# Decay sums by a prefix scan, first rows copied inside SBUF, later rows asked for an iteration ahead

## The chip, the cores and the metric

The kernel runs on one core of one Trainium2 chip. The metric is the device time of one execution in microseconds (us); a verdict compares medians of runs. TensorE (PE) does matmuls, with its weight loads in a queue of their own (PEld); VectorE is DVE, ScalarE is ACT, GpSimd is POOL. SyncE (SP) issues all DMAs here, in program order, one after the other.

## The reference

```python
scores = scale * np.matmul(q, k.transpose(0, 1, 3, 2))      # B=4, H=8, S=576, D=64
cum = np.cumsum(np.log(np.clip(f, 0.0001, 1.0)), axis=-1)
scores = np.where(causal, -1e9, scores + cum[:, :, :, None] - cum[:, :, None, :])
attn = softmax(scores)                                      # with 1e-9 in the denominator
x = (attn @ v), heads side by side                          # 2304 x 512
x = np.maximum(x @ w_in, 0.0) ** 2 @ w_out                  # d_ff 2048
out = (sigmoid(x @ w_gate) * (x @ w_val)) @ w_out2          # d_ff 1536
```

All inputs are float32; the running sum `cum` along the 576 positions of each of the 32 heads is the "decay sum" of the title. A row constant drops out of a softmax, so only `cum` of the key's position has to be added to the scores.

## The kernel before

The work has an attention part and, behind it, four passes of large matmuls for the two feed-forward layers. The attention part handles the 32 heads as 16 pairs. Each float32 operand of a matmul is split into a high and a low part (`qh`, `ql`, `kh`, `kl`), and a score block is the sum of `ql·kh`, `qh·kl`, `qh·kh` and of a fourth matmul that multiplies ones (`one_l`) with the tile `cr`: its rows 0, 1 and 64, 65 hold the high and low part of `cum` of the two heads. So no score block is complete before `cr` of its pair is there. `cr` exists twice, for even and odd pairs.

`setup()` runs once. It loads `f`, clips it (DVE), takes the logarithm (ACT, which then loads another table for Exp), and makes the running sum on TensorE: five transposes of `f` into `fT` (L242), then 14 matmuls with a triangle of ones (L256), evacuated in two pieces into `cum_s` (L261, L262), high and low. `cum_s` is written to `cum_d` in DRAM (L265). `cum_s`, `f_sb` and the triangle lie inside `pts`, a tile that later holds transposed probabilities.

A table, `ORDER`, fixes what every engine does in one iteration: each word is a step and a lag. `S01+0` are the first scores of this iteration's pair; `TQ-1` and `TK-1` transpose q and k of the next pair (L270); `qh`, `ql`, `kh`, `kl` split them on ACT and DVE; `R` (row minimum, DVE), `X` (exponential, ACT), `M` (scaling, POOL), `G` (transposes of the probabilities, PE), `E` (their evacuation) and `PV+2` (the product with v, L439) follow over the next two iterations. `TQ` and `TK` also issue the loads of q and k two pairs ahead, `PV` that of v three pairs ahead. `kh-1` issues the two DMAs that bring `cr` of the next pair from `cum_d` (L356): behind the loads of its own iteration on SP. The loads of v of pairs 0 to 2 are issued before the first iteration. A DMA on SP also waits for the DMA eight places ahead of it.

Of the kernel before, what the change touches and what calls it, by code (L numbers as in the profile page):

```python
# [9 lines left out]
F32 = mybir.dt.float32  # L10
F32R = mybir.dt.float32r
I32 = mybir.dt.int32
AF = mybir.ActivationFunctionType
ALU = mybir.AluOpType
# [26 lines left out]
def kernel(  # L41
# [13 lines left out]
    nc = tc.nc  # L55
    B, H, S, D = q.shape
    NT, DM = out.shape
    BH = B * H
    NP = BH // 2
    PB = H // 2  # L60
    NF = S // 128
    REM = S - NF * 128
    NC = NF + 1
# [6 lines left out]
    PC = S + 128 - REM  # L70
    POFF = [128 * (i * (i + 1) // 2) for i in range(NF + 1)]
# [4 lines left out]
    while t0 < NT:  # L76
        n = min(512, NT - t0)
# [5 lines left out]
    cum_d = dram.tile([BH, 2, S], F32, name="cum_d")  # L83
# [61 lines left out]
    def conv_load(n):  # L145
        for key, m, _, _ in conv_q[:n]:
            if (key, m) not in wraw:
                w_load(key, m)

    def conv_some(n):  # L150
        for _ in range(min(n, len(conv_q))):
            w_conv(*conv_q.pop(0))
            conv_load(3)
# [7 lines left out]
    def tiles(n, name, shape, dt=F32):  # L161
        return [ap_.tile(shape, dt, name=f"{name}{i}") for i in range(n)]

    nat = {nm_: tiles(3 if nm_ == "v" else 2, nm_ + "n", [128, NC, 2, D]) for nm_ in "qkv"}
    qk = [{nm_: ap_.tile([128, S], F32R, name=f"{nm_}{i}") for nm_ in ("qh", "ql", "kh", "kl", "cr")} for i in range(2)]
# [3 lines left out]
    pt_t = tiles(2, "pt", [128, 2 * POFF[NF] + PC])  # L169
    pts = ap_.tile([128, 2 * PW + 128], F32, name="pts")  # L170
    sm_t = tiles(2, "sm", [128, 9])
    nm_t = tiles(2, "nm", [128, 9])
    ident = ap_.tile([128, 128], F32, name="ident")
    MD = S + 384
    maskc = ap_.tile([128, MD + 128], F32, name="maskc")
    one_l = ap_.tile([128, 256], F32R, name="one_l")
    ones_f = pts[:, 0:S]
    f_sb = pts[0:BH, S:2 * S]
    cum_s = pts[0:BH, 2 * S:4 * S].bitcast(F32R)
    ones_u = qk[1]["kh"][:, 0:S]  # L180
    fT = qk[1]["kl"][:, 0:2 * NC * BH].rearrange("p (t c) -> p t c", t=2)

    ring = [0]

    def ps2():
        ring[0] += 1
        return pair_t[(ring[0] - 1) % 4]

    def load(p, which):
        b, h0 = divmod(2 * p, H)  # L190
        for src, nm_ in ((q, "q"), (k, "k"), (v, "v")):
            if nm_ not in which:
                continue
            t = nat[nm_][p % len(nat[nm_])]
            for i in range(2):
                nc.sync.dma_start(  # L196
                    out=t[:, 0:NF, i, :],
                    in_=src[b, h0 + i, 0:NF * 128, :].rearrange("(c p) d -> p c d", p=128),
                )
            nc.sync.dma_start(  # L200
                out=t[0:REM, NF, :, :],
                in_=src[b, h0:h0 + 2, NF * 128:S, :].rearrange("h p d -> p h d"),
            )

    def setup():
        nc.sync.dma_start(out=f_sb, in_=f.rearrange("b h s -> (b h) s"))
        for p in range(2):
            load(p, "qk")
        make_identity(nc, ident)
        nc.gpsimd.memset(ones_f, 1.0)  # L210
        nc.gpsimd.affine_select(
            out=ones_f, in_=ones_f, pattern=[[1, S]], compare_op=ALU.is_ge, fill=0.0, base=0, channel_multiplier=-1
        )
        for nm_ in "qkv":
            for t in nat[nm_]:
                nc.gpsimd.memset(t[64:128, NF, :, :], 0.0)
        nc.vector.tensor_copy(ones_u, ones_f)
        for d in qk:
            for nm_ in ("cr", "eh", "el"):
                nc.gpsimd.memset(d[nm_].bitcast(F32), 0.0)  # L220
        for t in pt_t:
            nc.gpsimd.memset(t[:, 2 * POFF[NF] + S:2 * POFF[NF] + PC], 0.0)
        nc.gpsimd.memset(one_l.bitcast(F32), 0.0)
        for r in range(2):
            nc.gpsimd.memset(one_l.bitcast(F32)[64 * r:64 * r + 2, 128 * r:128 * r + 128], 1.0)
        nc.gpsimd.memset(maskc, 0.0)
        nc.gpsimd.affine_select(
            out=maskc[:, MD:MD + 128], in_=maskc[:, MD:MD + 128], pattern=[[-1, 128]],
            compare_op=ALU.is_ge, fill=BIG, base=0, channel_multiplier=1,
        )  # L230
        for r in range(2):
            nc.gpsimd.affine_select(
                out=maskc[64 * r:64 * r + 64, S - REM:S], in_=maskc[64 * r:64 * r + 64, S - REM:S],
                pattern=[[-1, REM]], compare_op=ALU.is_ge, fill=BIG, base=0, channel_multiplier=1,
            )
        nc.vector.tensor_scalar(f_sb, f_sb, 1.0e-4, 1.0, op0=ALU.max, op1=ALU.min)
        nc.scalar.activation(out=f_sb, in_=f_sb, func=AF.Ln)
        nc.scalar.activation(out=sm_t[0][0:BH, 0:1], in_=f_sb[:, 0:1], func=AF.Exp)
        fps = ps2()
        for c in range(NC):  # L240
            n = 128 if c < NF else REM
            nc.tensor.transpose(fps[0:n, c * BH:(c + 1) * BH], f_sb[:, c * 128:c * 128 + n], ident[0:BH, 0:BH])  # L242
        for n, w0, w1 in ((128, 0, NF * BH), (REM, NF * BH, NC * BH)):
            nc.scalar.activation(out=fT[0:n, 0, w0:w1], in_=fps[0:n, w0:w1], func=AF.Copy)
            nc.vector.tensor_tensor(
                out=fT[0:n, 1, w0:w1], in0=fps[0:n, w0:w1], in1=fT.bitcast(F32)[0:n, 0, w0:w1], op=ALU.subtract
            )
        for a, e in ((0, 256), (256, S)):
            cps = ps2()
            for c in range(NC):  # L250
                n = 128 if c < NF else REM
                s = max(a, c * 128)
                if s >= e:
                    continue
                for t in range(2):
                    nc.tensor.matmul(  # L256
                        cps[0:BH, s - a:e - a], lhsT=fT[0:n, t, c * BH:(c + 1) * BH],
                        rhs=ones_u[0:n, s - c * 128:e - c * 128],
                        start=(c == 0 and t == 0), stop=(t == 1 and c == min(NF, (e - 1) // 128)),
                    )  # L260
            nc.scalar.activation(out=cum_s[:, a:e], in_=cps[0:BH, 0:e - a], func=AF.Copy)  # L261
            nc.vector.tensor_tensor(  # L262
                out=cum_s[:, S + a:S + e], in0=cps[0:BH, 0:e - a], in1=cum_s.bitcast(F32)[:, a:e], op=ALU.subtract
            )
        nc.sync.dma_start(out=cum_d, in_=cum_s.bitcast(F32).rearrange("p (t s) -> p t s", t=2))  # L265

    def transpose_in(t):
        x = ps2()
# [83 lines left out]
    def kh(p):  # L352
        d = qk[p % 2]
        nc.scalar.activation(out=d["kh"], in_=live["k", p], func=AF.Copy)
        for h in range(2):
            nc.sync.dma_start(out=d["cr"].bitcast(F32)[64 * h:64 * h + 2, :], in_=cum_d[2 * p + h, :, :])  # L356

    def kl(p):
        d = qk[p % 2]
# [87 lines left out]
    def x_part(p, low):  # L447
# [8 lines left out]
                nc.scalar.activation(out=x[:, 0, xs], in_=i, func=AF.Copy)  # L456

    STEP = {
        "TQ": TQ, "qh": qh, "ql": ql, "EH": EH, "EL": EL, "TK": TK, "kh": kh, "kl": kl,
        "S01": S01, "S2": S2, "S3": S3, "S4": S4, "PV": PV,  # L460
        "xhi": lambda p: x_part(p, 0), "xlo": lambda p: x_part(p, 1),
        "N0": lambda p: N(p, 0, 4), "N2": lambda p: N(p, 4, 6), "N3": lambda p: N(p, 6, 9),
    }
    for c in range(9):
        t = "4" if c == 8 else f"{c // 2}{'ab'[c % 2]}"
        for nm_, fn in (("R", R), ("X", expsum), ("M", M)):
            STEP[nm_ + t] = lambda p, fn=fn, c=c: fn(p, c)
    for g in range(1, 5):
        STEP[f"G{g}"] = lambda p, g=g: G(p, g)
        STEP[f"E{g}"] = lambda p, g=g: E(p, g)  # L470
    ORDER = """
        S01+0 M2a+1 X4+1 M1b+1 E3+2 R0a+0 R1b+0 X3b+1 PV+2 R0b+0 R1a+0 TQ-1 M2b+1 X3a+1
        xhi+2 S2+0 N3+1 qh-1 X0a+0 G1+1 M3b+1 X1b+0 xlo+2 TK-1 E1+1 ql-1 M3a+1 kh-1
        R2b+0 S4+0 X1a+0 X0b+0 R2a+0 X2a+0 G2+1 kl-1 G3+1 R4+0 E2+1 M4+1 EH-1 N0+0
        X2b+0 G4+1 E4+1 N2+0 S3+0 EL-1 M0b+0 M0a+0 M1a+0 R3b+0 R3a+0
# [2 lines left out]
    for m in range(2):  # L478
        conv_q.append(("in", m, ws_p, "wi"))

    setup()
    order = tc.manual_schedule()
    order.__enter__()
    for p in range(3):
        load(p, "v")
    steps = [(w[:-2], int(w[-2:])) for w in ORDER]
    lags = [lag for _, lag in steps]
    for it in range(min(lags), NP + max(lags)):
        for nm_, lag in steps:
            p = it - lag  # L490
            if 0 <= p < NP:
                STEP[nm_](p)
        if it == NP - 4:
            conv_load(2)
        if it in (NP, NP + 1):
            conv_some(1)
# [19 lines left out]
    def up(key, m, j):  # L516
        t0, n = blks[j]
        w = whl[key, m]
        h = hbank()
        for c in range(KD):  # L520
            x = xT[c][:, :, t0:t0 + n]
            wh, wl = w[:, 0, c * 128:(c + 1) * 128], w[:, 1, c * 128:(c + 1) * 128]
            for i, (a, b_) in enumerate(((wh, 0), (wh, 1), (wl, 0))):
                nc.tensor.matmul(  # L524
                    h[:, 0:n], lhsT=a, rhs=x[:, b_, :], start=(c == 0 and i == 0), stop=(c == KD - 1 and i == 2)
                )
        return h[:, 0:n]
# [11 lines left out]
    for m in range(M1):  # L539
        for j, (t0, n) in enumerate(blks):  # L540
            h = up("in", m, j)
# [109 lines left out]
```

## Time and profile before

| | us |
|---|---|
| three runs | 1053.26, 1053.84, 1054.04 (median 1053.84) |
| profiled execution, span from first to last instruction | 1051.2 |
| PE busy in it | 1027.0 |
| DVE / ACT / POOL busy | 503.3 / 399.5 / 220.7 |
| attention part, roughly | 0 to 209 of the span |

The profile has no time of its own beside its span; the median of the runs lies 2.64 us above the span. Read a row of the timeline as: start, duration (from the first of a merged group to the end of the last), engine, line, operation, out<-in, shape, count, and in brackets how long the engine had been idle and for what. A chain of waits is the work followed back from the last instruction to what released it.

### The profile page before, as it was taken

Reading aid. Unit: us, or ns where it says so; the run is one execution under the profiler, and the core shown is the slowest. Engines: PE = TensorE matmul, PEld = TensorE weight load, DVE = VectorE, ACT = ScalarE, POOL = GpSimd, SP = SyncE. Lnnn points to the kernel's source line nnn. Section 1 sums busy time; section 2 is a strip of 40 time slices with the busy share of each in tenths; the row PEclk is TensorE's granted clock in tenths of the full one; section 3 lists DMA queues with packets and bytes.
Section 4 is the critical chain, followed back from the end, with each engine's and each line's share of the span. In section 5 each row is a group of like instructions: output and inputs, shape, how many; then the busy total and the mean of one; then the engine's idle time right before and its main releaser. Section 6 shows DMA issues by size and latency. Waiting matters only on the chain.

```text
span 1051.2 us, 15632 instructions
## 1 busy us (share of the span) xinstructions
PE 1027.0 (98%) x5675; PEld 859.7 (82%) x5675; DVE 503.3 (48%) x1067; ACT 399.5 (38%) x854; POOL 220.7 (21%) x306
## 2 busy tenths in 40 slices
PE   4999999899999999999999999999999999999998
PEld 3788788588888888888888988888888888888887
DVE  2878778597666675233232414444444421232222
ACT  2888778544444343233232323222222211122222
POOL 3776666532122211000000002111111120000000
PEclk7999999899999999999999999999999999999999
DMA  5333333066765565333332214434433211244333
GB/s 121 71 86 87 70 83 106 21 187 199 210 211 188 188 204 167 101 93 98 101 93 83 85 51 119 132 124 132 132 119 107 94 46 46 78 138 140 99 123 110
DMA packets 125965, 121.98 MB, mean 116 GB/s; under 512 B 63552, under 2 KB 91200, under 8 KB 125888
## 3 DMA queue, kind: packets, MB, share of 16 engines
q1 hardware_dynamic: 125888, 120.99, 38.6%
q8 instruction: 44, 0.72, 0.3%
q14 instruction: 33, 0.27, 0.1%
HBM read 83.06 MB, written 37.90 MB: 115 GB/s over the span
## 4 chain that ended last, share of the span: by engine, by line
PE 95%; SPq 2%; DMA 1%; DVE 0%; issue 0%; ACT 0%; POOL 0%; POOLq 0%
PE ps L524 47%; PE ps L588 33%; PE pa L439 4%; PE pa L306 4%; PE pa L405 3%; PE pa L270 2%; PE pa L379 2%; SPq L196 1%; DMA cr<-cum_d 1%; PE pa L411 1%; SPq L200 1%; POOL pt L394 0%; ACT pt L292 0%; SPq L356 0%; ACT pts L316 0%
## 5 line engine op out<-in xcount | busy, mean ns | idle before, releaser
L524 PE MATMUL ps<-xT,hl 128*128 128x512 f32 (+1 forms) x2400 | 494.4, 368 | 0.0
L524 PEld LDWEIGHTS ps<-xT,hl 128*128 128x128 f32 x2400 | 418.4, 189 | 75.8
L141 POOL TENSOR_TENSOR hl<-wf,hl 128x512 fp32r<-128x512 f32 x68 | 93.1, 1377 | 565.1 <-ACT hl L140 548.6
L562 DVE TENSOR_TENSOR gg<-gi,gg 128x512 fp32r<-128x512 f32 (+1 forms) x140 | 90.5, 647 | 237.0 <-ACT gg L561 236.9
L588 PE MATMUL ps<-gg,hl 128*128 128x512 f32 (+1 forms) x960 | 197.3, 368 | 0.0
L588 PEld LDWEIGHTS ps<-gg,hl 128*128 128x128 f32 x960 | 167.2, 189 | 30.0
L561 ACT ACTIVATE gg<-gi 128x512 fp32r<-128x512 f32 (+1 forms) x140 | 82.4, 589 | 251.1 <-PE ps L588 227.8
L588 PE MATMUL ps<-hl,gg 128*128 128x512 f32 x648 | 147.1, 389 | 0.0
L588 PEld LDWEIGHTS ps<-hl,gg 128*128 128x128 f32 x648 | 121.6, 188 | 25.2
L394 POOL TENSOR_TENSOR pt<-pt,sm 128x128 f32<-128x128 f32 (+2 forms) x144 | 105.8, 767 | 53.8 <-DVE sm L389 53.8
L616 DVE TENSOR_TENSOR r<-ps,r 128x512 f32<-128x512 f32 (+1 forms) x60 | 38.2, 636 | 138.1 <-PE ps L524 133.3
L292 ACT ACTIVATE pt<-pt,nm 128x128 f32<-128x128 f32 (+1 forms) x144 | 82.5, 583 | 10.1 <-DVE nm L284 10.0
L137 DVE SCALAR_TENSOR_TENSOR wf<-wraw,wtmp 128x512 int32<-128x512 int32 x68 | 57.6, 848 | 57.4 <-POOL hl L141 56.0
L614 ACT ACTIVATE r<-ps 128x512 f32<-128x512 f32 (+1 forms) x60 | 32.9, 548 | 122.5 <-PE ps L524 122.5
L140 ACT ACTIVATE hl<-wf 128x512 fp32r<-128x512 f32 x68 | 42.9, 631 | 88.6 <-DVE wf L137 47.2
L131 ACT ACTIVATE wtmp<-wraw 128x512 f32<-128x512 f32 x68 | 45.2, 666 | 74.5 <-DMA wraw<-in_moe_w_in_dram 23.4
L284 DVE CUSTOM_DVE_ANT_0 pt<-pa,maskc 128x128 f32<-128x128 f32 (+2 forms) x144 | 67.0, 514 | 12.0 <-PE pa L306 11.4
L543 ACT ACTIVATE r<-ps 128x512 f32<-128x512 f32 (+1 forms) x80 | 42.5, 547 | 43.2 <-DMA g<-r 38.2
L544 DVE TENSOR_TENSOR r<-r 128x512 f32<-128x512 f32 (+1 forms) x80 | 50.7, 646 | 17.0 <-ACT r L543 17.0
L439 PE MATMUL pa<-pts,vn 128*64 128x320 f32 (+4 forms) x448 | 49.2, 371 | 3.9 <-ACT pts L316 3.9
L439 PEld LDWEIGHTS pa<-pts,vn 128*64 128x64 f32 x448 | 30.5, 141 | 22.9 <-ACT pts L316 4.4
L134 DVE SCALAR_TENSOR_TENSOR wtmp<-wraw,wtmp 128x512 int32<-128x512 int32 x68 | 48.0, 708 | 2.2
(79 smaller groups left out, 685.4 us busy)
## 6 DMA issues: line engine op xcount, KB each, us to landing
g<-r SPq DMA_DIRECT2D x112, 256.0 KB
gi<-g SPq DMA_DIRECT2D x112, 256.0 KB
wraw<-in_moe_w_out_dram SPq DMA_DIRECT2D x28, 512.0 KB
wraw<-in_moe_w_in_dram SPq DMA_DIRECT2D x16, 512.0 KB
wraw<-in_moe_w_gate_dram SPq DMA_DIRECT2D x12, 512.0 KB
wraw<-in_moe_w_val_dram SPq DMA_DIRECT2D x12, 512.0 KB
out_dram<-r SPq DMA_DIRECT2D x18, 256.0 KB
qn<-in_q_dram SPq DMA_DIRECT2D x32, 128.0 KB
```

The costliest lines, as they stand in the source:

```text
L134: nc.vector.scalar_tensor_tensor(out=xi, in0=hi, scalar=-0x40000000, in1=xi, op0=ALU.bitwise_and, op1=ALU.bitwise_or)
L137: nc.vector.scalar_tensor_tensor(out=t.bitcast(I32), in0=lo, scalar=29, in1=xi, op0=ALU.logical_shift_right, op1=ALU.bitwise_or)
L141: nc.gpsimd.tensor_tensor(out=hl[:, 1, :], in0=t, in1=hl.bitcast(F32)[:, 0, :], op=ALU.subtract)
L284: nc.vector.tensor_tensor_reduce(out=o, in0=s, in1=mask, scale=1.0, scalar=3.0e38, op0=ALU.add, op1=ALU.min, accum_out=nm_t[p % 2][:, c:c ...
L292: nc.scalar.activation(out=x, in_=x, func=AF.Exp, bias=nm_t[p % 2][:, c:c + 1], scale=-1.0, accum_out=sm_t[p % 2][:, c:c + 1])
L394: nc.gpsimd.tensor_tensor(out=x, in0=x, in1=sm_t[p % 2][:, c:c + 1].to_broadcast([128, e - a]), op=ALU.mult)
L439: nc.tensor.matmul(o[64 * h:64 * h + 64, 512 * half + s - lo:512 * half + hi - lo], lhsT=vn[:, c, h, :], rhs=pts[:, h * PW + c * PS + s:h ...
L524: nc.tensor.matmul(h[:, 0:n], lhsT=a, rhs=x[:, b_, :], start=(c == 0 and i == 0), stop=(c == KD - 1 and i == 2))
L544: nc.vector.tensor_tensor(out=r, in0=r, in1=r, op=ALU.mult)
L561: nc.scalar.activation(out=gg[:, 0, 0:n], in_=t, func=AF.Copy)
L562: nc.vector.tensor_tensor(out=gg[:, 1, 0:n], in0=t, in1=gg.bitcast(F32)[:, 0, 0:n], op=ALU.subtract)
L588: nc.tensor.matmul(o, lhsT=lhsT, rhs=rhs, start=(k_ == 0 and x == 0), stop=(last and x == 2))
```

## The change

Four things change.

The running sum is one DVE instruction: `tensor_tensor_scan` along the 576 positions of the 32 partitions, into `cum_f`, with the clamped logarithms as both operands. ACT copies it to the high half of `cum_s`, DVE subtracts for the low half. The transposes of `f`, the 14 matmuls, the triangle of ones and their evacuations are gone.

`cr` of pairs 0 and 1 is copied from `cum_s`, inside SBUF, in `cr_load`, with one DMA for the high rows of both heads and one for the low rows; it still leaves on SP. For later pairs a new step `CR-1` stands at the head of `ORDER` and reads `cum_d`; `kh` no longer issues these DMAs.

v of pairs 0 to 2 is loaded at the head of iterations 0 to 2. Clearing of tiles that are needed later (`eh`, `el` of the odd pairs, v, the probabilities) moves to `setup_late()`, called at the head of iteration 0. And `setup()` now stands inside the hand-written order, so that its instructions keep their written order too.

```diff
-        for p in range(2):
-            load(p, "qk")
...
+        load(0, "qk")
+        nc.vector.tensor_scalar(f_sb, f_sb, 1.0e-4, 1.0, op0=ALU.max, op1=ALU.min)
+        nc.scalar.activation(out=f_sb, in_=f_sb, func=AF.Ln)
+        nc.scalar.activation(out=sm_t[0][0:BH, 0:1], in_=f_sb[:, 0:1], func=AF.Exp)
+        nc.vector.tensor_tensor_scan(out=cum_f, data0=f_sb, data1=f_sb, initial=0.0, op0=ALU.add, op1=ALU.min)
+        nc.scalar.activation(out=cum_s[:, 0:S], in_=cum_f, func=AF.Copy)
+        nc.vector.tensor_tensor(
+            out=cum_s[:, S:2 * S], in0=cum_f, in1=cum_s.bitcast(F32)[:, 0:S], op=ALU.subtract
+        )
...
+        load(1, "q")
+        cr_load(0, cum_v)
+        load(1, "k")
+        cr_load(1, cum_v)
+        nc.sync.dma_start(out=cum_d, in_=cum_v)
...
-            nc.tensor.transpose(fps[0:n, c * BH:(c + 1) * BH], f_sb[:, c * 128:c * 128 + n], ident[0:BH, 0:BH])
...
-                        cps[0:BH, s - a:e - a], lhsT=fT[0:n, t, c * BH:(c + 1) * BH],
...
+    def cr_load(p, source):
+        d = qk[p % 2]
+        for t in range(2):
+            nc.sync.dma_start(out=d["cr"].bitcast(F32)[t:t + 65:64, :], in_=source[2 * p:2 * p + 2, t, :])
...
     def kh(p):
         d = qk[p % 2]
         nc.scalar.activation(out=d["kh"], in_=live["k", p], func=AF.Copy)
-        for h in range(2):
-            nc.sync.dma_start(out=d["cr"].bitcast(F32)[64 * h:64 * h + 2, :], in_=cum_d[2 * p + h, :, :])
...
-    for p in range(3):
-        load(p, "v")
...
+        if it == 0:
+            setup_late()
+        if 0 <= it < 3:
+            load(it, "v")
```

On SP, the stretch that ends with the first `cr` before. `vn` and `qn`, `kn` are the tiles of v, q and k; 228 to 230 are v of pairs 0 to 2, 224 and 226 belong to even pairs, 225 and 227 to odd ones; `cr_235` is that of even pairs. Ahead of the first row stand `f`, q and k of pairs 0 and 1 and v of pair 0.

```order
L196 DMA vn_229<-in_v_dram 128x4x64 x2
L200 DMA vn_229<-in_v_dram 64x2x64
L265 DMA cum_d<-pts 32x1152
L196 DMA vn_230<-in_v_dram 128x4x64 x2
L200 DMA vn_230<-in_v_dram 64x2x64
L196 DMA qn_224<-in_q_dram 128x4x64 x2
L200 DMA qn_224<-in_q_dram 64x2x64
L196 DMA kn_226<-in_k_dram 128x4x64 x2
L200 DMA kn_226<-in_k_dram 64x2x64
L356 DMA cr_235<-cum_d 2x576 x2
```

The same queue after the change, from q of pair 1 on. Ahead of the first row stand `f` and q and k of pair 0.

```order
L194 DMA qn_225<-in_q_dram 128x4x64 x2
L198 DMA qn_225<-in_q_dram 64x2x64
L206 DMA cr_235<-pts 2x576 x2
L194 DMA kn_227<-in_k_dram 128x4x64 x2
L198 DMA kn_227<-in_k_dram 64x2x64
L206 DMA cr_240<-pts 2x576 x2
L235 DMA cum_d<-pts 32x1152
L194 DMA qn_224<-in_q_dram 128x4x64 x2
L198 DMA qn_224<-in_q_dram 64x2x64
L194 DMA kn_226<-in_k_dram 128x4x64 x2
L198 DMA kn_226<-in_k_dram 64x2x64
L194 DMA vn_228<-in_v_dram 128x4x64 x2
```

The first `cr` moved from behind 29 loads and stores to behind 10; in its old place it also stood behind `cum_d`, from which it reads.

On PE, the head of the program before, up to the first scores of pair 0 (`pa` are PSUM tiles).

```order
L242 MATMUL pa_217<-ident,pts 128x32 x4
L242 MATMUL pa_217<-ident,pts 64x32
L270 MATMUL pa_220<-ident,qn_224 128x128 x3
L256 MATMUL pa_218<-kh_238,kl_239 32x256 x2
L256 MATMUL pa_218<-kh_238,kl_239 32x128 x2
L256 MATMUL pa_219<-kh_238,kl_239 32x320 x6
L256 MATMUL pa_219<-kh_238,kl_239 32x192 x2
L256 MATMUL pa_219<-kh_238,kl_239 32x64 x2
L270 MATMUL pa_220<-ident,qn_224 128x128 x2
L270 MATMUL pa_217<-ident,kn_226 128x128 x5
L306 MATMUL pa_218<-kh_233,ql_232 128x128 x2
```

And after the change.

```order
L262 MATMUL pa_217<-ident,qn_224 128x128 x5
L262 MATMUL pa_218<-ident,kn_226 128x128 x5
L298 MATMUL pa_219<-kh_233,ql_232 128x128 x2
L298 MATMUL pa_219<-kl_234,qh_231 128x128 x2
L298 MATMUL pa_219<-kh_233,qh_231 128x128 x2
L298 MATMUL pa_219<-cr_235,one_l 128x128 x2
```

The transposes of q of pair 0 are no longer cut in two by the matmuls of the running sum, and those of k follow at once.

## Rows read from the trace of the kernel before

**Rows 1.** The page, part 1: busy time of PE, share, instructions.

```profile
PE 1027.0 (98%) x5675; PEld 859.7 (82%) x5675; DVE 503.3 (48%) x1067; ACT 399.5 (38%) x854; POOL 220.7 (21%) x306
```

**Rows 2.** Waits, PE's and SP's: us in total, times, longest us.

```profile
PE pa L306 <- DMA cr<-cum_d: 10.4, 5, 8.7
...
SPq L196 <- PE pa L439: 66.0, 13, 7.7
```

**Rows 3.** Windows: us, busy of PE, PEld, DVE, ACT, POOL, clock, DMA share, GB/s.

```profile
12.00:20.00 8.00, 0.00 (x0) 0.00 (x0) 0.00 (x0) 0.00 (x0) 0.00 (x0) 0.52 0.71 161
20.00:26.00 6.00, 5.49 (x29) 4.53 (x30) 2.98 (x13) 1.52 (x5) 0.93 (x4) 0.50 0.21 48
```

**Rows 4.** Timeline of SP's queue, 0 to 20 us.

```profile
1.26 0.96 SPq L196 DMA_DIRECT2D qn<-in_q_dram  x2
...
3.02 1.14 SPq L196 DMA_DIRECT2D kn<-in_k_dram  x2
...
6.03 0.60 SPq L200 DMA_DIRECT2D qn<-in_q_dram  x1
...
18.34 0.74 SPq L356 DMA_DIRECT2D cr<-cum_d  x2
```

**Rows 5.** Timeline of ACT, DVE and PE, 0 to 21 us.

```profile
3.22 0.68 ACT L237 ACTIVATE pts<-pts 32x576 f32<-32x576 f32 x1 [1.13 <-DVE pts L236]
3.92 1.28 ACT L238 ACT_TABLE_LOAD   x1
...
4.94 0.87 PE L270 MATMUL pa<-ident,qn 128*128 128x128 f32 x3 [0.23 <-DMA qn<-in_q_dram]
5.21 0.20 ACT L238 ACTIVATE sm<-pts 32x1 f32<-32x1 f32 x1
...
9.79 0.65 ACT L354 ACTIVATE kh<-pa 128x576 fp32r<-128x576 f32 x1
...
10.60 0.75 DVE L360 TENSOR_TENSOR kl<-pa,kh 128x576 fp32r<-128x576 f32 x1
...
11.41 0.33 PE L306 MATMUL pa<-kl,qh 64*128 64x128 f32 x2 [0.25 <-DVE kl L360]
...
20.52 0.62 PE L306 MATMUL pa<-cr,one_l 64*128 64x128 f32 x2 [8.67 <-DMA cr<-cum_d]
```

**Rows 6.** Line L270 in three stretches (ns min/median/max, first to last start); timeline, 24.87.

```profile
L270 PE MATMUL pa<-ident,qn x3: 417/417/445, 4.9 to 5.4; 128*128 128x128 f32 x3
...
L270 PE MATMUL pa<-ident,kn x5: 272/273/273, 9.0 to 9.5; 128*128 128x128 f32 x5
...
L270 PE MATMUL pa<-ident,qn x5: 421/421/472, 22.0 to 22.9; 128*128 128x128 f32 x5
...
24.87 1.29 PE L270 MATMUL pa<-ident,kn 128*128 128x128 f32 x5
```

**Rows 7.** Timeline of PE and POOL around the second iteration.

```profile
29.36 0.54 PE L306 MATMUL pa<-cr,one_l 64*128 64x128 f32 x2 [0.74 <-DMA cr<-cum_d]
...
32.63 3.14 POOL L394 TENSOR_TENSOR pt<-pt,sm 128x512 f32<-128x512 f32 x3 [0.38 <-DVE sm L389]
...
35.89 0.71 PE L411 MATMUL pa<-ident,pt 128*128 128x128 f32 x5
```

**Rows 8.** Chain of waits: PV of pairs 0, 1, 2, 6 and 9.

```profile
38.64 2.85 PE pa L439 x28
...
50.43 2.85 PE pa L439 x28
...
61.41 2.86 PE pa L439 x28
...
105.56 2.86 PE pa L439 x28
...
140.62 2.86 PE pa L439 x28
```

More of the change, by code (lines that the diff above doesn't have):

```diff
@@ L176 @@
     one_l = ap_.tile([128, 256], F32R, name="one_l")
-    ones_f = pts[:, 0:S]
+    cum_f = pts[0:BH, 0:S]
     f_sb = pts[0:BH, S:2 * S]
     cum_s = pts[0:BH, 2 * S:4 * S].bitcast(F32R)
-    ones_u = qk[1]["kh"][:, 0:S]
-    fT = qk[1]["kl"][:, 0:2 * NC * BH].rearrange("p (t c) -> p t c", t=2)
     ring = [0]
@@ L203, in load @@
             )
+    def cr_load(p, source):
+        d = qk[p % 2]
+        for t in range(2):
+            nc.sync.dma_start(out=d["cr"].bitcast(F32)[t:t + 65:64, :], in_=source[2 * p:2 * p + 2, t, :])
     def setup():
         nc.sync.dma_start(out=f_sb, in_=f.rearrange("b h s -> (b h) s"))
-        for p in range(2):
-            load(p, "qk")
         make_identity(nc, ident)
[L210 to L214, printed above, removed]
+        for nm_ in "qk":
             for t in nat[nm_]:
                 nc.gpsimd.memset(t[64:128, NF, :, :], 0.0)
-        nc.vector.tensor_copy(ones_u, ones_f)
+        load(0, "qk")
[7 more added lines that the diff above has]
+        )
         for d in qk:
[L219 to L222, printed above, removed]
+            nc.gpsimd.memset(d["cr"].bitcast(F32), 0.0)
+        for nm_ in ("eh", "el"):
+            nc.gpsimd.memset(qk[0][nm_].bitcast(F32), 0.0)
         nc.gpsimd.memset(one_l.bitcast(F32), 0.0)
@@ L225, in setup @@
             nc.gpsimd.memset(one_l.bitcast(F32)[64 * r:64 * r + 2, 128 * r:128 * r + 128], 1.0)
+        cum_v = cum_s.bitcast(F32).rearrange("p (t s) -> p t s", t=2)
+        load(1, "q")
[3 more added lines that the diff above has]
+        nc.sync.dma_start(out=cum_d, in_=cum_v)
         nc.gpsimd.memset(maskc, 0.0)
@@ L235, in setup, with setup_late, CR @@
             )
[L236 to L241, printed above, removed]
-            nc.tensor.transpose(fps[0:n, c * BH:(c + 1) * BH], f_sb[:, c * 128:c * 128 + n], ident[0:BH, 0:BH])
[L243 to L256, printed above, removed]
-                        cps[0:BH, s - a:e - a], lhsT=fT[0:n, t, c * BH:(c + 1) * BH],
[L258 to L265, printed above, removed]
+    def setup_late():
+        for nm_ in ("eh", "el"):
+            nc.gpsimd.memset(qk[1][nm_].bitcast(F32), 0.0)
+        for t in nat["v"]:
+            nc.gpsimd.memset(t[64:128, NF, :, :], 0.0)
+        for t in pt_t:
+            nc.gpsimd.memset(t[:, 2 * POFF[NF] + S:2 * POFF[NF] + PC], 0.0)
+    def CR(p):
+        if p > 1:
+            cr_load(p, cum_d)
     def transpose_in(t):
@@ L458 @@
     STEP = {
-        "TQ": TQ, "qh": qh, "ql": ql, "EH": EH, "EL": EL, "TK": TK, "kh": kh, "kl": kl,
+        "CR": CR, "TQ": TQ, "qh": qh, "ql": ql, "EH": EH, "EL": EL, "TK": TK, "kh": kh, "kl": kl,
         "S01": S01, "S2": S2, "S3": S3, "S4": S4, "PV": PV,
@@ L471 @@
     ORDER = """
-        S01+0 M2a+1 X4+1 M1b+1 E3+2 R0a+0 R1b+0 X3b+1 PV+2 R0b+0 R1a+0 TQ-1 M2b+1 X3a+1
+        CR-1 S01+0 M2a+1 X4+1 M1b+1 E3+2 R0a+0 R1b+0 X3b+1 PV+2 R0b+0 R1a+0 TQ-1 M2b+1 X3a+1
         xhi+2 S2+0 N3+1 qh-1 X0a+0 G1+1 M3b+1 X1b+0 xlo+2 TK-1 E1+1 ql-1 M3a+1 kh-1
@@ L479 @@
         conv_q.append(("in", m, ws_p, "wi"))
-    setup()
     order = tc.manual_schedule()
     order.__enter__()
-    for p in range(3):
-        load(p, "v")
+    setup()
     steps = [(w[:-2], int(w[-2:])) for w in ORDER]
```

## The prediction

> **What bounds the kernel now.** I read the page first: PE is busy 98% of the span [rows 1], so time is won only where PE stands still or runs slowly. The waits come next: the longest of PE's is for `cr`, 10.4 us in five waits, one of them 8.7 us [rows 2]. [...] SP's queue says why: the two DMAs of the first `cr` are issued at 18.34, the last of a row of loads of which most are for later pairs [rows 4]; the matmul that needs them starts at 20.52 [rows 5]. So the first 20 us are bounded by SP's order. One column has to be read with care: the windows give a clock of 1.00 ahead of 12 us, but a transpose takes 417 ns at 4.9 us and 421 at 22 us, where the clock is 0.50, against 273 at 9 us [rows 6]. PE begins the program on the low level. After that, `cr` is late again by 0.74 us at 29.36 [rows 7], and in single iterations later: PV starts are normally 10.98 us apart (50.43 to 61.41), but 11.79 from pair 0 to 1, and 35.06 for the three from pair 6 to 9 [rows 8]. The chain of waits runs through a `cr` DMA there.
>
> **The change part by part.** I count against the span of 1051.2; the median of the runs lies 2.64 above it, and differences carry over.
>
> The running sum. The logarithm ends at 3.90, and from then the scan can run on DVE [rows 5]. The trace has no scan. The nearest rows of this length are 0.68 (ACT, 576 long) and 0.75 (DVE, 576 long), so it is hardly under 0.5; upward I allow four such times, 3 us. I take about 1 us, close to these rows. ACT isn't free before 5.41 anyhow: it loads the Exp table until 5.20 and does the small Exp after it [rows 5]. A scan of up to 1.5 us therefore costs nothing. Then the copy (0.68, as the logarithm) to 6.09 and the subtraction (at most 0.75) to 6.84.
>
> [...]
>
> The first `cr`. Its place on SP is behind q of pair 1, whose last issue ends at 6.63 [rows 4]. The first DMA leaves then, the second after the subtraction, so both are out by 7.3. Before, it took 2.18 us from the first issue (18.34) to the matmul (20.52). So `cr` lands at 8.8 to 9.1.
>
> q and k of pair 0. The transposes of q still start at 4.94, when the load has landed: 3.68 us after its first issue at 1.26 [rows 4, 5]. They are no longer cut by the matmuls of the sum. Five at the low clock take 1.29 [rows 6], so to 6.3, and `qh` follows on ACT behind the copy, to 6.95. k is issued at 3.02; with the same 3.68 it is there at 6.7, and its transposes end at 8.0. `kh` (0.65) ends at 8.7, `kl` (0.75) at 9.5 [rows 5]. With `kl` ready the next two groups of matmuls took 0.44 before (11.41 to 11.85, the 8.67 us ahead of 20.52 [rows 5]); `cr`'s matmul comes at 10.0. So k, not `cr`, is late last, by about 1 us, and that matmul moves from 20.52 to 10.0: **10.5 us**. Bounds: k's transposes did run at 9.0 before [rows 6], so k was there by then; with 1.29 for them and the same steps `cr`'s matmul comes at 12.3, a gain of 8.2. Were k no limit, `cr`'s landing gives 11.7.
>
> The clock. PE does little before 9.6 in the new kernel, and it begins on the low level [rows 6]. Before, it worked on the low level from 20.5 to 26, 5.5 us after its restart [rows 3]. I carry that stretch over unchanged: 0, with 1 us either way, as the rise may come sooner or later after the restart.
>
> [...] Going by the column, a clock that is high from the start would bring the sum 2.7 us more; that is a rival below.
>
> The wait at 29.36. `cr` of pair 1 is now issued behind k of pair 1, at about 9.2, and needed at 28.6 - 10.5 = 18.1, so the 0.74 us [rows 7] go. But what comes next in that iteration is POOL: its scaling ends at 35.77 and the transposes that need it start at 35.89 [rows 7]. DVE and ACT in front of POOL don't wait for this `cr`. PE can move up by 0.12 only; I credit **0.1**, with bounds 0 and 0.74.
>
> The later waits. `CR-1` leaves at the head of the iteration before its use, some 11 us ahead, against a landing of 2.18. The excess of the PV starts goes: 11.79 - 10.98 = 0.8, and 35.06 - 32.94 = 2.1 [rows 8]; some 0.2 more is spread over the periods between. **3.1 us**, bounds 0 and 3.2. From the third iteration PV adds 2.85 us of PE work [rows 8], so POOL is no longer as close behind.
>
> What is moved and priced at nothing. v of pair 0 now leaves at about 14 us, behind q and k of pair 2, and with 3.68 lands by 20; PV of pair 0 needs it at 38.64 - 10.6 = 28. Without that cover every us of lateness would cost one. k of pair 1 leaves at about 7.4, its last piece lands by 12.5; its transposes come at 24.87 - 10.5 = 14.4. That is the tightest, with 2 us. `CR` waits on SP for the last scores of two pairs ago, and v, q and k stand behind it; but SP already waits 66.0 us in 13 times for PV [rows 2], some 5 us an iteration, so the queue has room. The clearings that move to `setup_late` lie on POOL, which is idle between 12 and 20 [rows 3] and has no work in that place now.
>
> Sum: 10.5 + 0.1 + 3.1 = 13.7. The span becomes 1037.5, the median 1040.1. All behind the attention part is PE work that starts that much earlier.
>
> **The rivals.**
> 1. k (or a scan beyond 3 us, which holds ACT and with it `qh` and `kh`) is later than I reckon: gain 8.2 + 0.1 + 3.1 = 11.4, 1042.4. For it: transposes of k were not seen before 9.0. Against it: q's 3.68.
> 2. The later waits stay or turn into others (q or k landing late, POOL): 10.5 + 0.1 and up to 0.5, 1042.9. For it: the DMAs of an iteration are the same in number, and POOL's 0.12. Against it: 11 us of lead.
> 3. The clock is high from the start, as the column says, and in pair 0 PE loses nothing: half of 5.5, 2.7 more, 1037.4. Against it: 417 ns.
> 4. Slower: `CR`, at the head of SP's queue and waiting for PE, holds back q and k of later pairs until PE waits for them. Its place is each of 14 iterations; it decides from 13.7 / 14 = 1.0 us in each, and at 1.3 us gives 1058. The loads would have to be some 10 us later than now; 5 us of slack an iteration speak against it.
> 5. No change: what was won at the head is lost at the start of the feed-forward part, if weights or stores bound that; 1053. PE's 98% speaks against it.
>
> **How the numbers follow.** My forecast 0.62, the rivals 0.12, 0.10, 0.10, 0.03, 0.03. A measurement of this kernel can tell about 0.2% (2.1 us) from no change. Faster by more than that: the forecast and rivals 1 to 3, 0.94; within it 0.03; slower 0.03. The range takes in rivals 1 to 3 with a us for the clock: 1036.6 to 1043.7.
>
> **What would show it.** In the new profile the first matmul with `cr` should start at 10.0, with `kl` and not the DMA as what it waited for; the transposes of q should take some 420 ns each; the scan should end before 5.4. PE should be busy without a gap of a us from there to the end of the attention part, on the low clock for about 5 us of it; the wait for `cr` should be gone from the list of waits; the period of PV should be 10.98 throughout, and the first PV about 10.6 earlier. Wrong would be: a `cr` DMA that lands after 9.5, a gap at 12 to 15 for k of pair 1, a new wait of PE for POOL or ACT in the second iteration of more than 0.7.

## The result, and the profile after

The changed kernel takes 1038.26 us in the median (four runs, 1037.49 to 1039.14); the kernel before, beside it, 1053.61. The ratio is 0.9852 with a 95% interval of 0.9838 to 0.9866: 15.4 us less. The forecast was 1040.1, with a range of 1036.6 to 1043.7. The profiled execution went from a span of 1051.2 to 1037.2, where 1037.5 was forecast.

The head first. The timeline of PE, ACT, DVE and SP after the change, merged rows, answers to [rows 4] and [rows 5]:

```profile
4.20 1.28 ACT L217 ACT_TABLE_LOAD   x1
4.22 1.35 DVE L218 TENSOR_TENSOR_SCAN pts<-pts 32x576 f32<-32x576 f32 x1 [0.75 <-ACT pts L216]
4.51 1.30 PE L262 MATMUL pa<-ident,qn 128*128 128x128 f32 x5 [4.51 <-DMA qn<-in_q_dram]
...
6.31 0.75 DVE L220 TENSOR_TENSOR pts<-pts 32x576 fp32r<-32x576 f32 x1 [0.75 <-ACT pts L219]
6.61 1.30 PE L262 MATMUL pa<-ident,kn 128*128 128x128 f32 x5 [0.80 <-DMA kn<-in_k_dram]
6.75 1.25 SPq L206 DMA_DIRECT2D cr<-pts  x2
...
8.63 0.76 DVE L350 TENSOR_TENSOR kl<-pa,kh 128x576 fp32r<-128x576 f32 x1 [0.90 <-ACT kh L346]
...
9.44 0.47 PE L298 MATMUL pa<-kl,qh 64*128 64x128 f32 x2 [0.32 <-DVE kl L350]
...
9.93 0.42 PE L298 MATMUL pa<-cr,one_l 64*128 64x128 f32 x2
```

The last row has no bracket: the first matmul with `cr` starts at 9.93 instead of 20.52, straight behind the others, and waits for nothing. What PE did wait for is in the row of 9.44: `kl`, 0.32 us.

The list of PE's waits, us in total, times, longest, answers to [rows 2] (the first six of seven; the last is that for `kl`):

```profile
PE pa L262 <- DMA qn<-in_q_dram: 4.5, 1, 4.5
PE pa L429 <- ACT pts L308: 3.9, 1, 3.9
PE pa L262 <- DMA kn<-in_k_dram: 0.8, 1, 0.8
PE pa L298 <- ACT kh L346: 0.7, 1, 0.7
PE pa L395 <- POOL pt L384: 0.7, 1, 0.7
PE pa L369 <- DVE ql L323: 0.7, 1, 0.7
```

The row for `cr`, 10.4 us before, is gone. The wait for q is the time until the first load lands, when PE begins; the one of L429 for ACT lies ahead of the last PV and was there before (3.9). The chain of waits, PV of pairs 0, 1 and 13, answers to [rows 8]:

```profile
27.92 2.85 PE pa L429 x28
...
38.90 2.85 PE pa L429 x28
...
170.66 2.85 PE pa L429 x28
```

The last of the same rows before:

```profile
184.57 2.85 PE pa L439 x28
```

From 27.92 to 170.66 are 13 periods of 10.98, to the last digit; before, the same two rows (38.64 and 184.57) stood 145.93 apart, 3.19 more. So the 14.0 us of the span are 10.59 at the first `cr` matmul, 0.13 from there to the first PV, 3.19 in the 13 periods after, and 0.1 at the end. The profiled execution is one of the longer ones: the four have spans of 1037.2, 1035.7, 1037.4 and 1035.7, and where the 1.5 us between them lie is told below, under the clock.

### The profile page after: what moved, and what is told of

It reads as the page before. It is cut to its first block, busy times and chain, and to the rows that moved or that the text cites. A ratio compares the mean times of both kernels' runs of the same rounds, so it can differ in the third digit from the quotient of the medians.

```text
span 1037.2 us, 15625 instructions
## 1 busy us (share of the span) xinstructions
PE 1021.9 (99%) x5656; PEld 856.8 (83%) x5656; DVE 504.3 (49%) x1064; ACT 399.4 (39%) x851; POOL 220.2 (21%) x304
## 4 chain that ended last, share of the span: by engine, by line
PE 98%; DVE 1%; ACT 0%; DMA 0%; SPq 0%; POOL 0%; issue 0%
PE ps L516 48%; PE ps L580 33%; PE pa L429 5%; PE pa L298 4%; PE pa L395 3%; PE pa L262 2%; PE pa L369 2%; PE pa L401 1%; DMA kn<-in_k_dram 0%; DVE pt L276 0%; ACT pt L284 0%; POOL pt L384 0%; SPq L194 0%; ACT kh L346 0%; ACT pts L308 0%
## 5 line engine op out<-in xcount | busy, mean ns | idle before, releaser
L429 PE MATMUL pa<-pts,vn 128*64 128x320 f32 (+4 forms) x448 | 49.1, 371 | 3.9 <-ACT pts L308 3.9
L429 PEld LDWEIGHTS pa<-pts,vn 128*64 128x64 f32 x448 | 30.5, 141 | 22.7 <-ACT pts L308 4.2
L132 DVE TENSOR_SCALAR wtmp<-wtmp 128x512 f32<-128x512 f32 x68 | 39.1, 576 | 20.6 <-ACT wtmp L131 20.4
```

The source lines that it names most:

```text
L429: nc.tensor.matmul(o[64 * h:64 * h + 64, 512 * half + s - lo:512 * half + hi - lo], lhsT=vn[:, c, h, :], rhs=pts[:, h * PW + c * PS + s:h ...
```

## Experiments

All against the kernel before on the same chip: e1 to e4 ran on one chip, e5, e7 and e8 on a second, e0, e6, e10 and e11 on a third. Spans are those of the one profiled execution of each; the changed kernel alone has spans from 1035.6 to 1037.4, so a difference of spans under about 1.5 us is read together with the medians.

| kernel | median, us | ratio, interval | span |
|---|---|---|---|
| changed (second measurement, e0) | 1038.0 | 0.9857 (0.9842 to 0.9871) | 1035.7 |
| e1 later rows behind k again | 1053.16 | 1.0002 (0.9988 to 1.0016) | 1049.9 |
| e8 the same, one DMA a head | 1046.72 | 0.9946 (0.9931 to 0.9961) | 1044.9 |
| e2 sum on PE again | 1041.1 | 0.9894 (0.9877 to 0.991) | 1038.7 |
| e3 scan alone | 1052.6 | 0.9998 (0.9989 to 1.0007) | 1052.4 |
| e4 v by pairs alone | 1047.85 | 0.9952 (0.9937 to 0.9967) | 1046.5 |
| e6 first rows through DRAM | 1039.98 | 0.9872 (0.9855 to 0.9888) | 1039.0 |
| e7 first rows three DMAs later | 1039.72 | 0.9876 (0.9859 to 0.9892) | 1038.0 |
| e5 extra matmuls at the head | 1038.3 | 0.9862 (0.9847 to 0.9877) | 1035.5 |
| e5 extra transposes at the head | 1037.78 | 0.9857 (0.9843 to 0.9872) | 1035.0 |
| e10 PE filled, conversion earlier | 1040.1 | 0.9878 (0.9863 to 0.9893) | 1037.8 |
| e11 conversion earlier | 1040.03 | 0.9876 (0.9861 to 0.989) | 1038.1 |

**e3: the scan alone, on the kernel before.**

```diff
-            nc.tensor.transpose(fps[0:n, c * BH:(c + 1) * BH], f_sb[:, c * 128:c * 128 + n], ident[0:BH, 0:BH])
...
-                    nc.tensor.matmul(
...
+        nc.vector.tensor_tensor_scan(out=cum_f, data0=f_sb, data1=f_sb, initial=0.0, op0=ALU.add, op1=ALU.min)
+        nc.scalar.activation(out=cum_s[:, 0:S], in_=cum_f, func=AF.Copy)
+        nc.vector.tensor_tensor(
...
```

> The kernel before with one change: the running sum is the scan. SP's order stays. Theory: the first rows are late because of their place behind the loads on SP, so nothing is won: first matmul with the rows at 20.2 to 20.6, time within 0.3 us of the kernel before. Rival: the matmuls of the sum were what delayed the start; several us are won.

The sums are ready sooner, and nothing comes of it. Timeline of SP and PE:

```profile
8.54 0.51 SPq L239 DMA_DIRECT2D cum_d<-pts  x1
...
18.31 0.75 SPq L330 DMA_DIRECT2D cr<-cum_d  x2
...
20.30 0.62 PE L280 MATMUL pa<-cr,one_l 64*128 64x128 f32 x2 [10.37 <-DMA cr<-cum_d]
```

The store left 3.7 us earlier than before, the rows at 18.31 against 18.34: their place in the queue sets the time, as the theory had it. The span is 1.2 us longer, but no more than single executions differ: the later waits for rows came out larger here (13 periods of PV took 147.74, from 38.37 to 186.11, against 145.93 before), and the medians are equal within their interval.

**e4: v pair by pair alone, on the kernel before.**

```diff
-    for p in range(3):
-        load(p, "v")
...
+        if 0 <= it < 3:
+            load(it, "v")
```

> The kernel before with one change: v of pairs 0 to 2 is loaded at the head of iterations 0 to 2. The nine DMAs leave SP's queue ahead of the first rows. Theory: the store of the sums then waits for the sum (9.7), q and k of pair 2 follow, the rows are issued at 14.0 and used at 16.2: 4.3 us won at the head, the later waits stay; span about 1046.9. Rival: the DMA engines, not SP's order, were the limit; then the rows come hardly earlier, under 1 us won.

```profile
10.21 0.45 SPq L265 DMA_DIRECT2D cum_d<-pts  x1
...
13.35 0.74 SPq L356 DMA_DIRECT2D cr<-cum_d  x2
...
15.12 0.86 PE L306 MATMUL pa<-cr,one_l 64*128 64x128 f32 x2 [2.71 <-DMA cr<-cum_d]
```

The rows' matmul came 5.4 us earlier, and the span fell by 4.7 (5.2 in the medians), as the theory had it. The later waits stayed and came out somewhat larger: PV of pairs 0, 1 and 2 started at 33.70, 45.81 and 57.77, 12.11 and 11.96 apart where it had been 11.79 and 10.98, and 13 periods took 147.04. That the v loads are the reason isn't shown: in e3, where v stands as before, the 13 periods took 147.74. Nor did these loads push on the queue here: the first of them (14.13 to 15.74) and the third (30.90 to 32.49) were followed by 2.3 and 4.0 us in which SP waited for PE.

**e2: the sum on PE again, all else as changed.** (Edit: the reverse of e3, on the changed kernel.)

> The changed kernel, with the running sum made on PE again (transposes of f, triangle, 14 matmuls, evacuations), all else as changed. Theory: k of pair 0 is last at the head, so what the scan buys is that PE is free for the transposes of q and k: these now stand behind the sum, whose last evacuation ended at 9.7 before, and the first matmul with the rows comes at 13.3 instead of 9.9; the span is about 3.4 us longer. Rival: SP's order alone makes the head's gain, the scan buys nothing; the first matmul with the rows comes at about 10 to 10.5 and the span is under 0.6 us longer.

The first matmul with the rows came at 12.51, 2.6 us later than with the scan; 3.4 was expected. The clock then gave nearly all of it back. The five transposes of q of pair 1, here and in the changed kernel:

```profile
13.24 0.76 PE L290 MATMUL pa<-ident,qn 128*128 128x128 f32 x5
```

```profile
11.23 1.33 PE L262 MATMUL pa<-ident,qn 128*128 128x128 f32 x5
```

With the matmuls of the sum PE has worked 6.8 us from 4.20 on when q of pair 1 comes, and its five transposes take 0.76 us; without them it has worked 4.9 from 4.51 on, and they take 1.33. By the wait for `ql` in the next iteration only 0.23 us of the 2.6 were left (22.68 against 22.45). Then came a wait that the changed kernel does not have. The chain of waits of e2 from there to the first PV:

```profile
22.68 1.35 PE pa L397 x8
...
26.19 0.52 SPq L208
...
26.75 1.90 DMA cr<-cum_d
...
28.79 0.85 PE pa L326 x10
29.64 2.86 PE pa L457 x28
```

The first rows leave SP when the sum is ready, at 9.45 and not 6.75, and all that stands behind them leaves 2.7 us later too. So the rows of pair 2 left at 26.19 (23.46 in the changed kernel), and PE stood for them until 28.79. The first PV came 1.7 later, and the span was 1.5 longer; in the medians it is about 3 us (1041.1 against 1038.26 and 1038.0), as the profiled execution of e2 is the shortest of its four. The scan is worth that much, but in these two traces most of it is SP's queue running earlier, not PE's path at the head.

**e6: the first rows through DRAM.**

```diff
         load(1, "q")
-        cr_load(0, cum_v)
+        nc.sync.dma_start(out=cum_d, in_=cum_v)
+        cr_load(0, cum_d)
         load(1, "k")
-        cr_load(1, cum_v)
-        nc.sync.dma_start(out=cum_d, in_=cum_v)
+        cr_load(1, cum_d)
```

> The changed kernel with the first two sets of decay rows read from DRAM: the store of the sums is issued where the first rows were, and the rows behind it read what it wrote. Theory: the store has to land (about 2 us) before SP issues the rows, and the rows then land some 1.5 to 2 us later; the first matmul with them comes at 11.5 to 12.3 instead of 9.9, the span is 1.6 to 2.4 us longer. Rival: the round trip is hidden behind k, as the rows have 1 us to spare; under 0.6 us longer.

```profile
7.08 0.34 SPq L232 DMA_DIRECT2D cum_d<-pts  x1
...
9.16 1.14 SPq L206 DMA_DIRECT2D cr<-cum_d  x2
...
11.93 0.48 PE L298 MATMUL pa<-cr,one_l 64*128 64x128 f32 x2 [2.00 <-DMA cr<-cum_d]
```

SP stands from 7.42, when the store is out, to 9.16, when the rows that read it leave. The matmul comes 2.0 us later, the span is 1.8 longer (the median 2.0 above e0, on the same chip): that is what reading straight from SBUF buys.

**e7: how much the first rows have to spare.** (Edit: `cr_load(0, cum_v)` moved below `load(1, "k")`.)

> The changed kernel with the first decay rows issued behind k of pair 1 instead of ahead of it, so 1.8 us later. Theory: the rows have about 1 us to spare because k is late last; the first matmul with them moves from 9.9 to 10.6 to 11.0, the span grows by 0.7 to 1.1. Rival: the rows themselves set the start; it moves by the full 1.8.

```profile
8.57 2.33 SPq L206 DMA_DIRECT2D cr<-pts  x4
...
11.04 0.48 PE L298 MATMUL pa<-cr,one_l 64*128 64x128 f32 x2 [0.95 <-DMA cr<-pts]
```

Issued 1.82 us later, the rows moved their matmul by 1.11 (9.93 to 11.04) and the span by 0.8. So they had 0.7 us to spare, as 2.47 from issue to use says too: 6.75 + 2.47 = 9.2. k was last.

**e1 and e8: the later rows behind k again.** In e1 `CR-1` is gone and `kh` issues the rows, in the new form (one DMA for the same row of both heads); in e8 in the old form (one for both rows of a head).

```diff
         nc.scalar.activation(out=d["kh"], in_=live["k", p], func=AF.Copy)
+        CR(p)
...
-        CR-1 S01+0 M2a+1 X4+1
+        S01+0 M2a+1 X4+1
```

> The changed kernel, with the decay rows of pairs 2 to 15 asked for where they stood before, behind k of the same iteration. Theory: the later waits for these rows cost about 3 us, and asking an iteration ahead is what took them away. They come back: the span is 2 to 3.2 us longer than 1037.2, the first matmul with the rows still starts at 9.9, and PE again waits for the rows in single iterations from 40 us on. Rival: those waits went because the whole program starts earlier or because v is loaded later; then the span stays within 0.5 us of 1037.2.

> As the kernel with the rows of pairs 2 to 15 behind k of the same iteration, but with the DMAs of before (one for both rows of a head, instead of one for the same row of both heads). Theory: that kernel lost 12.7 us and not 3 because the new form takes 0.5 us to issue instead of 0.35 and lands later, and the loop PV, v, q, k, rows, scores was already as long as PE's own period of 10.98; with the old form the span is 2 to 4 us above 1037.2. Rival: it is the place alone; the span stays at about 1050.

e1 missed its number by far. Its span is 12.7 us longer than that of the changed kernel, and its ten runs (1049.37 to 1057.78) have the median of the kernel before: the whole gain is gone, with the first matmul at 9.70. The first PV came at 30.82, 2.9 later than in the changed kernel, and the 13 periods behind it took 9.45 more. PE's waits, the chain (two PV) and SP's queue in between:

```profile
PE pa L298 <- DMA cr<-cum_d: 10.1, 12, 3.1
```

```profile
54.60 2.86 PE pa L430 x28
...
66.23 2.86 PE pa L430 x28
```

```profile
57.36 0.92 SPq L194 DMA_DIRECT2D vn<-in_v_dram  x2
58.38 0.66 SPq L198 DMA_DIRECT2D vn<-in_v_dram  x1
59.13 1.09 SPq L194 DMA_DIRECT2D qn<-in_q_dram  x2
60.31 0.64 SPq L198 DMA_DIRECT2D qn<-in_q_dram  x1
61.05 1.09 SPq L194 DMA_DIRECT2D kn<-in_k_dram  x2
62.23 0.60 SPq L198 DMA_DIRECT2D kn<-in_k_dram  x1
62.88 1.07 SPq L206 DMA_DIRECT2D cr<-cum_d  x2
```

It is a loop: the load of v waits for PV (57.36 is about the end of the PV that began at 54.60), q, k and the rows stand behind it on SP, the scores wait for the rows, and the next PV for the scores. In e1 it takes 11.63 us here, more than PE's own 10.98, and eleven of the 13 periods pay, 0.5 to 2.0 us each. In the kernel before the loop was just as long as PE's period:

```profile
64.17 0.95 SPq L196 DMA_DIRECT2D vn<-in_v_dram  x2
...
69.64 0.75 SPq L356 DMA_DIRECT2D cr<-cum_d  x2
```

The same seven rows took 6.22 us (from 64.17 to 70.39) against 6.59 in e1, and only single iterations paid, 3.2 us in all. The new form costs 0.5 us an issue against 0.33, and its rows are used later: 2.50 us from the first issue to the matmul that waited (62.88 to 65.38) against 1.70 (47.67 to 49.37, before). All issues of the rows in e1, then those in the kernel before (behind the colon shortest, median and longest in ns):

```profile
L206 SPq DMA_DIRECT2D cr<-cum_d x28: 457/498/527, 27.4 to 177.0; - x28
```

```profile
L356 SPq DMA_DIRECT2D cr<-cum_d x32: 243/330/447, 18.3 to 178.5; - x32
```

e8 tests that: with the old form the span is 5.0 us shorter than e1's (the median 6.4), so the form is part of it, but 7.7 longer than the changed kernel's, not 2 to 4. Of these, 3.1 lie in the 12 periods from pair 1 on (43.31 to 178.14), which is what the later waits had cost before. One wait makes up much of the rest, in the third iteration:

```profile
28.95 0.78 PE L300 MATMUL pa<-cr,one_l 64*128 64x128 f32 x2 [2.96 <-DMA cr<-cum_d]
```

The rows of pair 2 left at 27.38 there, behind q, k and v of several pairs issued without a break since 15 us, six of these loads being v of pairs 0 and 1; PE was slower behind that wait, and the next PV took 4.34 us instead of 2.85. The first PV came 2.5 later for it, and the second another 1.9. The theory on the form holds; that it was all beside the known 3 us does not. That the six loads of v are what made these rows late is argued from the queue; no run takes them away there.

**e5: PE kept busy at the head.** (Edit: transposes or matmuls of the identity into a free PSUM tile, ahead of q's and k's transposes and the first scores.)

> The changed kernel with nine extra matmuls of the identity with itself on PE, into a PSUM tile that is free then: six ahead of the transposes of q of pair 0, two ahead of those of k, one ahead of the first scores; nothing else is touched. Theory: PE starts on the low clock and stays on it until 15.4, which costs about 2 us in pair 0; kept busy from 1.3 us on it is on the high level by 10 us at the latest, transposes of q of pair 1 take 273 ns instead of 421, the first PV starts 1.5 to 2.6 us earlier and the span is that much shorter (1034.6 to 1035.7). Rival: behind PE, DVE and ACT are next in pair 0 (or k of pair 1 has not landed), so a faster PE only waits: under 0.5 us won.

> As the kernel with extra matmuls, but with 15 transposes of the identity in their place (ten, three, two). Theory: any PE work releases the clock, so the result is that of the extra matmuls within 0.5 us. Rival: transposes don't count as activity; the clock rises at about 15 us as in the changed kernel and nothing is won.

Both raise the clock, and both lose it again. With extra matmuls the five transposes of k took 0.74 us (at 6.45) and those of q of pair 1 1.33 (at 10.60); with extra transposes it was the same:

```profile
6.39 0.74 PE L262 MATMUL pa<-ident,kn 128*128 128x128 f32 x5 [0.27 <-DMA kn<-in_k_dram]
...
10.55 1.33 PE L262 MATMUL pa<-ident,qn 128*128 128x128 f32 x5
```

PE waited 0.52 and 0.47 us for `kh` and `kl` in between. The first PV came at 26.48 (transposes) and 27.18 (matmuls), 1.4 and 0.7 earlier than in the changed kernel's profile. But the head of e11 below is that of the changed kernel, unaltered, and its first PV came at 26.87, that of e0 at 27.51: the head differs by as much from run to run. In the medians neither can be told from the changed kernel (1037.78 and 1038.3 against 1038.26 and 1038.0). That transposes alone raise the clock is shown by the 0.74, against 1.30 in the changed kernel: up to there PE had done nothing else.

**e10 and e11: an attempt at a faster version.** e11 converts the first tile of `w_in` two iterations earlier, to take it from ahead of the last PV (`if it in (NP - 2, NP + 1): conv_some(1)`); e10 does that and fills PE at the head more closely.

> The changed kernel with the earlier conversion alone. Theory: PE's wait of 3.9 us ahead of the last PV and the low clock behind it go, 4 to 6 us won, span 1031 to 1033. Rival: the conversion makes PE wait as long in the iteration into which it moves: within 1 us of 1037.

> A version meant to be faster: the changed kernel with extra matmuls of the identity that fill PE's idle stretches at the head (six ahead of the transposes of q, three ahead of those of k, three and one around the first matmuls of the first scores), and with the conversion of the first tile of w_in done two iterations earlier, so that the evacuation ahead of the last PV no longer stands behind it on ACT. Theory: the clock stays high from about 6 us on (2 to 3 us won in pair 0), and PE's wait of 3.9 us for the evacuation and the low clock behind it go (4 to 6 us won): span 1028 to 1031. Rival: DVE and ACT are next in pair 0 and the conversion only moves the wait to the attention part: span above 1034.

Neither won anything. e11's median is 2.0 us above e0's and e10's 2.1, so the rivals had the mechanism right (e11's span of 1038.1 lies just outside its "within 1 us of 1037"). In e11 the wait moved and grew:

```profile
PE pa L429 <- ACT pts L308: 5.4, 1, 5.4
```

The conversion stands in ACT's queue ahead of the exponentials and the evacuation of that iteration and waits there for DVE, 4.66 us here and 4.81 in its old place:

```profile
172.66 0.63 ACT L140 ACTIVATE hl<-wf 128x512 fp32r<-128x512 f32 x1 [4.66 <-DVE wf L137]
```

At e10's head the clock did stay high (q of pair 1: `10.03`, 0.76 for five), but the first PV came at 26.93 only; a new wait had come:

```profile
PE pa L298 <- DMA cr<-cum_d: 1.8, 1, 1.8
```

The rows of pair 2 left SP at 23.66 there, behind v of pair 1, much as in the changed kernel (23.46), and PE stood for them until 26.08. As in e2, these rows are what comes next when PE's head is early. No version that clearly beats the changed kernel was found.

## Why the prediction was right, point by point

**The head.** Right, and for the reason given. k, not `cr`, was last: transposes of k at 6.61 (6.7 forecast), `kl` done at 9.39 (9.5), the matmul at 9.93 (10.0), and e7 shows that the rows alone had 0.7 us to spare (1 forecast). Some terms were mis-sized, and k's lateness covered it: the scan took 1.35 us, not 1 (the subtraction of the same shape took 0.75), and the clipping ahead of it 0.81 instead of 0.51, so the scan ended at 5.57, not before 5.4, and ACT's copy began at 5.61 instead of 5.41; and the two `cr` DMAs took 1.25 us to issue and were out by 8.0, not 7.3.

**The clock.** Right in that PE starts low: the transposes of q and k took 1.30 for five, against 0.77 at 18.48, though the windows read a clock of 1.00 for all of the first 20 us there. The low stretch lasted till about 15.4 (a matmul of 288 columns took 0.54 us at 15.05 and 0.30 at 15.43), 5.5 us after 9.93, as carried over. That it came out so exactly is luck: the same head stayed low till about 15.9 in e0 (288 columns: 0.44 at 15.52, 0.29 at 15.96) and till about 13.1 in e11 (two matmuls of 384 columns: 0.49 at 12.82, 0.35 at 13.14), and its first PV came at 27.92, 27.51 and 26.87. The allowance of 1 us either way was needed.

The prediction has no term for a second low stretch. Ahead of the last PV, PE stands 3.9 us for ACT, in both kernels (so it was not "without a gap of a us"), and the granted clock is low behind that wait (0.50 from 190 to 194 us here, from 204 to 210 before). The last PV in the profile of the changed kernel, and in e0's:

```profile
191.09 4.32 PE pa L429 x20
```

```profile
190.68 3.59 PE pa L429 x20
```

From 194 to 196 us the granted clock is 0.50 in the first and 1.00 in the second. Of the 1.5 us between these two spans, 0.4 are there by the first PV, 0.7 in this PV, and 0.4 in the first matmuls behind it. This is also more than half of the distance between the forecast and the median: the median of the four spans lies 1.05 below the forecast's 1037.5. The rest is the offset of the median to the span: 2.64 was taken from the runs of before, while the runs whose span is known lie 1.8 above it.

**The wait at 29.36.** The size came out (0.1 forecast, 0.13 measured), but from the first matmul with `cr` to the first PV the same program took 17.99, 17.74 (e0) and 17.09 us (e11), so the agreement is luck, and the name was only half right. It isn't POOL that comes next in the second iteration but DVE: the chain of waits runs from `kh` of pair 1 through ACT and DVE to `ql`, and PE waits 0.66 for it:

```profile
22.45 0.40 PE L369 MATMUL pa<-kh,el 128*128 128x288 f32 x1 [0.66 <-DVE ql L323]
```

**The later waits.** The forecast was 3.1, the measurement 3.19, and the reason holds: with the rows behind k again, in the old form, e8 lost 3.1 in its periods from pair 1 on. The size rests on one trace, though: with the rows in the same place and form the 13 periods took 145.93 before, 147.74 in e3 and 147.04 in e4. And the step that priced `CR-1` by these waits alone was too simple. In the changed kernel, rows behind k cost 7.7 us in the old form (e8) and 12.7 in the new one (e1), not 3. Asking early is the cover under which the new form of the DMAs was free, and under which the head could start 10.6 us sooner without PE standing 3 us for the rows of pair 2. The prediction named a cover for v's own use, not for what v may push back on SP.

**The rivals.** None decided. k landed in time; the clock was not high from the start; `CR` did wait on SP, 20.9 us in twelve times, but SP's waits for PV fell from 66.0 to 30.7, so the queue had the room; and from the last PV's end to the end of the span it took 841.8 us, 841.9 before, so nothing was lost in the feed-forward part. The parts do not add up. By the profiled spans (medians in brackets): scan alone nothing, v alone 4.7 (5.2), without the scan 1.5 missing (3), without the SBUF source 1.8 (2.0), without the early asking 12.7 (15).

What stays open: what decides how long the clock stays low, at the head and behind the wait of 3.9 us, no run shows. No run takes the move of v, or that of the clearings, out of the changed kernel.

## What to carry over

When a first transfer is late, look at what stands ahead of it in its queue before making its source faster: here the faster sum alone won nothing, and moving v alone won a third of the whole; with the queue in order, the sum was then worth 1.5 to 3 us. A queue that holds loads which wait for an engine, and small transfers on which that engine waits, is a loop; compare its length with the engine's own period, since on the edge a little more costs it nearly every time: with 11.63 us (in one iteration) against 10.98, eleven of 13 periods paid (e1). And before pricing a moved load at nothing, ask what else it now stands ahead of.

## What the runs showed of the hardware

A DMA that fills row t of two heads (two partitions 64 apart) took 0.5 us to issue (e1), one that fills two neighbouring rows 0.33 (before); their sources in DRAM differ as well, two pieces against one, so which side costs it is not shown. Between a store to DRAM and the reads of it SP stood for 1.7 us (e6). Transposes alone raised PE's clock: behind 18 of them, five of k took 0.74 us instead of 1.30 (e5). And the work that the scan took from PE was not all time saved: with the sum's matmuls five transposes of q of pair 1 took 0.76 us, without them 1.33, and of the 2.6 us that they cost at the first matmul with `cr` only 0.2 were left an iteration later (e2).
